# One 1024-column tile for the decays of all eight heads, and one two-bank PSUM tile for both score banks

## The chip, the cores and the metric

The kernel runs on one core of a Trainium2 chip. The metric is the device time of one execution in microseconds (us); the time before is 815.35 us, the median of 3 runs (815.07 to 815.9).

## What is computed

An mLSTM attention over 4 batches, 8 heads, 768 positions and head size 40, and behind it two feed-forward layers over its 3072 tokens of 320 numbers (2048 hidden units).

```python
for t in range(S):                                  # attention, per batch and head
    m_new  = maximum(f_gate[t] + m, i_gate[t])
    f_stab = exp(f_gate[t] + m - m_new); i_stab = exp(i_gate[t] - m_new); m = m_new
    C = f_stab * C + i_stab * outer(v[t], k[t])
    n = f_stab * n + i_stab * k[t]
    y[t] = sigmoid(o_gate[t]) * (C @ q[t]) / maximum(abs(n @ q[t]), 1.0)
x = y.transpose(0, 2, 1, 3).reshape(3072, 320)
h = x @ moe_w_in;  x = (h - tanh(h)) @ moe_w_out    # layer 0
h = x @ moe2_w_in                                   # layer 1: 0 below -1, h above 1,
g = where(h >= 1, h, where(h <= -1, 0, (h + 1) ** 2 / 4))   # a parabola between
out = g @ moe2_w_out
```

## The kernel before

The sequence is cut into chunks of 128 positions. A **job** n = 0 to 23 is one chunk c = n // 4 of one batch b = n % 4, with all 8 heads in two halves u = 0, 1 of four heads (512 columns). The 24 jobs make six blocks of four; block k of the first feed-forward layer needs the results of jobs 4k to 4k+3. Each layer runs 6 blocks of 16 **steps**; a step f multiplies the block's 512 columns by 128 hidden units (L650, `h`), applies the activation (L668 ACT tanh, L669 DVE subtraction, L681 ACT rounding to `gh`, L682 DVE remainder `gl`), and two steps later (LAG) multiplies the result into four accumulators (L702, `a`). In block 0 the first eight steps use plain fp32 matmuls (L640). Jobs of later blocks are interleaved with the steps of layer 0.

What a job does, in order: it loads q and k (`qkraw`), k, v and o (`nat`) and, for jobs 4 and later, the row of decay factors of each head broadcast over 128 partitions (`fb`, two DMAs of 256 KB); L460 turns each half of `fb` into a 128x128 matrix of decays per head by a scan against repeated identity matrices (`scan_id`), into a buffer `d`; L463 copies the last column of each to `wc`, which POOL (L506) multiplies into k; PE makes the scores of the two halves (`t_s`, L473 for jobs below 12, L489 from 12 on, where L484 and L486 first split q and k into two parts, through one buffer `xf`, one half at a time); L493 multiplies each bank of scores by its half of `d`; L520 multiplies q, scaled by `gb` on POOL (L510, L512), by the running state `C` into `t_n`; L529 adds the scores times v; L536 to L546 normalise; L551 transposes into `t_x`; L601 to L606 (`split_x`) leave the result in two parts for layer 0; L558 makes the new outer products `t_c`, L566 to L575 the new state.

PSUM has eight banks: two with the tag `h` for the steps, four accumulators `a0` to `a3`, and `tn` and `tb`. From job 4 on a job uses `tn` for `s0`, `n` and `x` one after the other and `tb` for `s1` and `c`; the gates' small transpose `t_i` (L370) takes `tn`. In layer 1 four steps run as a group whose `h` banks are h, h, `tn` and `tb`. `fb` has two buffers of 512 columns and `d` three.

The order of instructions on every engine is fixed when the program is built, by a list planner (`Plan`) with its own costs. Each operation has an engine, a cost in ns and a priority (`prio`, a lower one first); the planner always places the operation that can start earliest, and among those of one engine that could start within 150 ns of it the one of lowest priority. A buffer or bank of a tag comes free when its last user has ended, and is given out in the order in which the program asks for it. Operations with `lock` don't overlap in the plan, since DVE and POOL share a port. All loads go through the queue of SP, in order: a load that waits for its buffer holds those behind it. A job of block k has the priority 16(k-1) + 4(n mod 4) - 6 + s for its stage s, a step the number of the step, a step's activations that number less 3.5.

Of the kernel before, what the change touches and what calls it, by code (L numbers as in the profile page):

```python
# [7 lines left out]
F32 = mybir.dt.float32  # L8
# [10 lines left out]
L = 128  # L19
# [35 lines left out]
FFN = 4  # L55
STACK = 12
GS = 4
HTAGS = ["h", "h", "tn", "tb"]


class Buf:
# [14 lines left out]
class Plan:  # L76
# [20 lines left out]
    def op(self, eng, ns, prio, fn, r=(), w=(), out=None, lock=False):  # L97
        o = Op()
        o.eng, o.ns, o.prio, o.fn, o.seq, o.out = eng, ns, prio, fn, len(self.ops), out
        o.allocs, o.preds, o.succs = [], set(), []  # L100
        o.bufs, o.fill, o.lock = [], 0, lock
        key = lambda x: x if isinstance(x, tuple) else (x, None)

        for x in map(key, r):
# [3 lines left out]
        for x in map(key, w):  # L108
# [5 lines left out]
        for b in {key(x)[0] for x in (*r, *w)}:  # L114
# [99 lines left out]
def dve(n):  # L214
    return 157 + n / 0.96
# [16 lines left out]
def mlstm_moe_moe(ctx: ExitStack, tc: tile.TileContext, ig, fg, qk, qk3, q3, nat, w1, w2, cst, out):  # L232
# [7 lines left out]

    cs = const.tile([128, C_W], F32, name="cs")
    ident = cs[:, C_ID:C_ID + 128]
    scan_id = const.tile([128, 512], F32, name="scan_id")
    scan_bf = scan_id.bitcast(BF16)
# [32 lines left out]
    BANKS = {"h": 2}  # L277

    def bank(tag, name):
        return P.buf(of(ps), [128, 512], F32, tag, name, BANKS.get(tag, 1))  # L280

    def load(prio, dst, src, kb, r=(), w=(), rows=None, eng="SP"):

# [56 lines left out]
    def gates(g, prio):  # L340
        ca, cb = GROUPS[g]
        n = (cb - ca) * L
        cols = slice(ca * L, cb * L)
        if g == 0:
            fr, i_sb, m_sb, gr = (wbuf(NF - 1 - i, [128 if i == 0 else B * H, 2 * L + 1], F32, "gate0") for i in range(4))
        else:
            fr, i_sb, m_sb, gr = (abuf(t, [B * H, L + 1], F32, 1) for t in ("fr", "ig", "mg", "gr"))
        gt[g] = fr, gr
        ld = prio - 4 if g else -99
        load(ld, lambda: fr[0:32, 0:n], lambda: fg[:, cols], n / 8, w=[fr], rows=n * 4)  # L350
        load(ld, lambda: i_sb[0:32, 0:n], lambda: ig[:, cols], n / 8, w=[i_sb], rows=n * 4, eng="ACT" if g == 0 else "SP")
        op("DVE", 60, prio, lambda: nc.vector.tensor_copy(m_sb[:, 0:1], carry[:, g:g + 1]), [("carry", g)], [m_sb])
        op("DVE", dve(2 * n), prio, lambda: nc.vector.tensor_tensor_scan(
            out=m_sb[:, 1:n + 1], data0=fr[0:32, 0:n], data1=i_sb[:, 0:n],
            initial=carry[:, g:g + 1], op0=ALU.add, op1=ALU.max), [fr, i_sb, m_sb, ("carry", g)], [m_sb])
        if g + 1 < len(GROUPS):
            op("DVE", 60, prio, lambda: nc.vector.tensor_copy(carry[:, g + 1:g + 2], m_sb[:, n:n + 1]), [m_sb], [("carry", g + 1)])
        for o, d, f in ((fr, 0, ALU.add), (fr, 1, ALU.subtract), (i_sb, 1, ALU.subtract)):
            def part(e, o=o, d=d, f=f):
                z = o[0:32, 0:n]  # L360
                e.tensor_tensor(out=z, in0=z, in1=m_sb[:, d:n + d], op=f)

            vec(prio, n, part, [o, m_sb], [o])
            if d:
                x = op("ACT", act(n) + (1283 if o is fr and g else 0), prio, lambda o=o: nc.scalar.activation(o[0:32, 0:n], o[0:32, 0:n], AF.Exp), [o], [o])
                if g == 0:
                    exps.append(x)
        t = bank("h" if g == 0 else "tn", "t_i")
        for c in range(cb - ca):
            op("PE", pe(32), prio, lambda c=c: nc.tensor.transpose(  # L370
                t[:, c * 32:c * 32 + 32], i_sb[:, c * L:(c + 1) * L], ident[:32, :32]), [i_sb, "cs"], [t])
        op("DVE", dve(32 * (cb - ca)), prio, lambda: nc.vector.tensor_copy(
            isT[:, ca:cb, :], t[:, 0:(cb - ca) * 32].rearrange("p (c h) -> p c h", h=32)), [t], [("isT", g)])
# [3 lines left out]
    def decays(g, prio):  # L377
# [14 lines left out]
        load(max(prio, -60), lambda: fr_d[:, cols], lambda: fr[0:32, z], 16, [fr], [("fr_d", g)], rows=512)  # L392
        load(max(prio, -60), lambda: gr_d[:, cols], lambda: gr[:, z], 16, [gr], [("gr_d", g)], rows=512)

    def jbank(n, what, name):

        tag = {"s0": "tn", "s1": "tb", "n": "tn", "x": "tn", "c": "tb", "f": "h"}[what]
        if n < FIRST and what in "s0s1xc":
            tag = (("a3", "tb"), ("a0", "a1"))[n % 2][what in ("s1", "x")]
        return bank(tag, name)  # L400


    Cst = {}
# [2 lines left out]
    def job(n, at, ld):  # L406
# [14 lines left out]
        kc = group[c]  # L421
        f = {}
        if n >= FIRST:
            for u in range(2):
                ft = abuf("fb", [128, HU, L], F32, 2)
                load(ld + 0.5, lambda ft=ft: ft.t, lambda u=u: fr_d[
                    b * H + u * HU:b * H + (u + 1) * HU, c * L:(c + 1) * L].unsqueeze(0).to_broadcast([128, HU, L]),
                    256, r=[("fr_d", kc)], w=[ft], rows=512)
                f[u] = lambda ft=ft: ft.t.rearrange("p h t -> p (h t)"), ft
        if c > 0:  # L430
            g = abuf("gb", [120, 3, L], F32, 2)
            for i in range(3):
# [9 lines left out]
        dk = {}  # L442
        d0 = wbuf(6 + n % 2, [128, 1024], F32, "d0") if n < FIRST else None
        wc = abuf("wc", [128, H], F32, 2)
        for u in range(2):
            p = at(0) if u == 0 else at(1)
            if n < FIRST:
                ft = jbank(n, "f", "t_f")
                for h in range(HU):
                    r = b * H + u * HU + h  # L450
                    op("PE", 2 * pe(L, 128, 2), p, lambda h=h, r=r, ft=ft: nc.tensor.matmul(
                        ft[:, h * L:(h + 1) * L], ident[:, r:r + 1].to_broadcast([128, 128]),
                        gt[0][0][:, 0:L], start=True, stop=True), [gt[0][0], (gt[0][0], "z", 32), (gt[0][0], "z", 64), "cs"], [ft])
                f[u] = lambda ft=ft: ft.t, ft
            if d0 is None:
                d = abuf("d", [128, 512], F32, 3)
                dk[u] = lambda d=d: d.t, d
            else:
                dk[u] = lambda u=u: d0[:, u * 512:(u + 1) * 512], (d0, u)
            op("DVE", dve(1024), p, lambda o=dk[u][0], i=f[u][0]: nc.vector.tensor_tensor_scan(  # L460
                out=o(), data0=i(), data1=scan_id, initial=0.0, op0=ALU.mult, op1=ALU.add), [f[u][1], "scan_id"], [dk[u][1]], lock=n >= FIRST)
# [17 lines left out]
        else:  # L479
            for u in range(2):  # L480
# [7 lines left out]
                for h in range(HU):  # L488
                    op("PE", pe(L), at(u + 0.5), lambda u=u, t=t, h=h: nc.tensor.matmul(  # L489
                        sp[u][:, h * L:(h + 1) * L], t[:, 512 + h * L:512 + (h + 1) * L],  # L490
                        t[:, h * L:(h + 1) * L], start=True, stop=True), [t], [sp[u]])
        for u in range(2):
            op("DVE", dve(512), at(2 + u), lambda p=sp[u], d=dk[u][0]: nc.vector.tensor_tensor(  # L493
                out=d(), in0=p.t, in1=d(), op=ALU.mult), [sp[u], dk[u][1]], [dk[u][1]])

# [279 lines left out]
    def reload(f, prio):  # L775
# [157 lines left out]
```

## Time and profile before

| | |
|---|---|
| median of 3 runs | 815.35 us (815.07 to 815.9) |
| the profiled execution | 814.9 us, its span 813.1 us |
| PE (TensorE matmul) busy | 803.5 us, 99% of the span |
| DVE, ACT, POOL busy | 570.3, 429.6, 147.5 us |
| granted clock of TensorE | 1.000 |

The span runs from the first to the last instruction; the profiled execution took 1.8 us more than its span. Jobs 0 to 3 and the first loads fill about the first 33 us, layer 0 with the later jobs lies between 33 and about 460 us, layer 1 behind it. A busy PE is not a PE at its peak, since matmuls are pipelined and their ends are modelled; how far it is from waiting is read from the stretch between the starts of successive groups of matmuls.

### The profile page before, as it was taken

To read this page: it belongs to the slowest core of one execution; us is meant where nothing else is said; L and a number is where in the kernel's file an instruction comes from. 1 tells how busy PE (TensorE), PEld (TensorE's weight loads), DVE (VectorE), ACT (ScalarE), POOL (GpSimd) and SP (SyncE) were. 2 spreads that over 40 slices of the span, in tenths; PEclk is the share of its full clock that TensorE was granted. 3 is DMA by queue.
4 is the path that set the end of the run, shared out by engine and by line. 5 is a ranking of instruction groups with operands and counts; after the bars stand their busy time and mean duration, and the time that the engine had idled before them with its cause. 6 is when DMAs were issued, how large, how long until landed. Compare 5 with 4: busy or idle time off the path is not lost.

```text
span 813.1 us, 15218 instructions
## 1 busy us (share of the span) xinstructions
PE 803.5 (99%) x6030; PEld 692.8 (85%) x6034; DVE 570.3 (70%) x922; ACT 429.6 (53%) x810; POOL 147.5 (18%) x147
## 2 busy tenths in 40 slices
PE   9999999999999999999999999999999999999998
PEld 6656888888898888888899888898888889898887
DVE  6899989878888998887456684554646555564644
ACT  4866775675586677544455553443525435342432
POOL 3242122314234335332110200200200201000000
PEclk9999999999999999999999999999999999999999
DMA  8888356686758768771543120100100000000000
GB/s 263 311 261 271 101 194 175 165 260 160 202 164 243 206 188 230 214 178 45 150 116 100 53 72 1 40 33 1 40 33 1 32 1 1 33 1 1 34 1 32
DMA packets 62980, 93.66 MB, mean 115 GB/s; under 512 B 4701, under 2 KB 45501, under 8 KB 62909
## 3 DMA queue, kind: packets, MB, share of 16 engines
q1 hardware_dynamic: 62860, 92.66, 39.2%
q8 instruction: 47, 0.77, 0.4%
q14 instruction: 25, 0.20, 0.1%
q10 hardware_dynamic: 48, 0.03, 0.0%
HBM read 78.88 MB, written 13.80 MB: 114 GB/s over the span
## 4 chain that ended last, share of the span: by engine, by line
PE 90%; DMA 3%; DVE 2%; issue 1%; ACT 1%; SPq 1%; POOL 0%; POOLq 0%; ACTq 0%
PE a L702 40%; PE h L650 37%; PE h L640 3%; PE t_n L529 2%; PE h L629 2%; PE t_n L520 1%; PE t_s L473 1%; PE t_c L558 1%; PE t_s L489 1%; DMA nat<-in_nat_dram 1%; PE t_x L551 1%; DMA w_d<-w 1%; SPq L286 1%; DMA gb<-gr_d 1%; DMA fr_d<-fr 0%
## 5 line engine op out<-in xcount | busy, mean ns | idle before, releaser
L650 PE MATMUL h<-x,w 128*128 128x512 f32 x1376 | 350.1, 397 | 0.1
L702 PE MATMUL a<-w,gh 128*128 128x320 f32 x1472 | 329.3, 310 | 0.0
L650 PEld LDWEIGHTS h<-x,w 128*128 128x128 f32 x1376 | 249.5, 188 | 52.2 <-issue 6.8
L702 PEld LDWEIGHTS a<-w,gh 128*128 128x128 f32 x1472 | 250.0, 188 | 11.0 <-ACT ob L725 1.8
L702 PE MATMUL a<-w,gl 128*128 128x320 f32 x736 | 227.5, 310 | 0.0
L673 DVE TENSOR_SCALAR g<-h 128x512 f32<-128x512 f32 x96 | 63.7, 684 | 114.1 <-PE h L650 114.1
L675 ACT ACTIVATE g<-g,half 128x512 f32<-128x512 f32 x96 | 67.0, 721 | 135.5 <-DVE g L673 135.0
L702 PEld LDWEIGHTS a<-w,gl 128*128 128x128 f32 x736 | 138.2, 188 | 0.3
L669 DVE TENSOR_TENSOR h<-h,g 128x512 f32<-128x512 f32 x88 | 61.2, 695 | 44.0 <-ACT g L668 43.9
L677 DVE TENSOR_TENSOR g<-h,g 128x512 f32<-128x512 f32 x96 | 64.7, 692 | 27.1 <-ACT g L675 26.1
L681 ACT CAST gh<-g 128x512 fp32r<-128x512 f32 x96 | 59.5, 622 | 44.3 <-DVE g L677 43.6
L668 ACT ACTIVATE g<-h 128x512 f32<-128x512 f32 x88 | 52.5, 597 | 53.4 <-PE h L650 52.8
L766 POOL TENSOR_TENSOR x<-xl,x 128x512 fp32r<-128x512 f32 x18 | 25.0, 1420 | 278.1 <-ACT x L757 278.1
L681 ACT CAST gh<-h 128x512 fp32r<-128x512 f32 x88 | 51.4, 585 | 45.3 <-DVE h L669 45.0
L682 DVE TENSOR_TENSOR gl<-h,gh 128x512 fp32r<-128x512 f32 x88 | 60.1, 683 | 19.1 <-ACT gh L681 17.3
L682 DVE TENSOR_TENSOR gl<-g,gh 128x512 fp32r<-128x512 f32 x96 | 62.1, 687 | 4.0 <-ACT gh L681 1.2
L460 DVE TENSOR_TENSOR_SCAN d<-fb,scan_id 128x512 f32<-128x512 f32 x40 | 54.6, 1376 | 1.9 <-DMA fb<-fr_d 1.8
L486 POOL TENSOR_TENSOR xf<-qkraw,xf 120x1024 fp32r<-120x1024 f32 x12 | 32.6, 2713 | 38.1 <-ACT xf L484 34.4
L484 ACT ACTIVATE xf<-qkraw,cs 120x512 fp32r<-120x512 f32 x48 | 32.5, 716 | 6.1 <-PE t_s L489 6.0
L493 DVE TENSOR_TENSOR d<-t_s,d 128x512 f32<-128x512 f32 x48 | 32.0, 681 | 4.4 <-PE t_s L489 2.9
L539 POOL TENSOR_TENSOR nat<-nat,dn 128x320 f32<-128x320 f32 x24 | 21.0, 874 | 70.3 <-DVE dn L538 70.3
L500 POOL TENSOR_TENSOR nat<-nat,isT 128x328 f32<-128x328 f32 x24 | 22.6, 952 | 57.9 <-DMA nat<-in_nat_dram 37.2
(103 smaller groups left out, 765.2 us busy)
## 6 DMA issues: line engine op xcount, KB each, us to landing
w<-in_w_dram SPq DMA_DIRECT2D x32, 703.6 KB
nat<-in_nat_dram SPq DMA_DIRECT2D x24, 484.0 KB
qkraw<-in_qk_dram SPq DMA_DIRECT2D x24, 480.0 KB
fb<-fr_d SPq DMA_DIRECT2D x40, 256.0 KB
w_d<-w SPq DMA_DIRECT2D x16, 352.0 KB
w<-w_d SPq DMA_DIRECT2D x16, 352.0 KB
qkraw<-in_qk_dram SPq DMA_DIRECT2D x24, 160.0 KB
xr_d<-xo SPq DMA_DIRECT2D x24, 160.0 KB
```

What stands on the lines that cost most here:

```text
L460: op("DVE", dve(1024), p, lambda o=dk[u][0], i=f[u][0]: nc.vector.tensor_tensor_scan(out=o(), data0=i(), data1=scan_id, initial=0.0, op0=A ...
L484: op("ACT", act(512, 1), at(u - 1), lambda raw=raw, t=t, z=z, cols=cols: nc.scalar.activation(t[:, cols], raw[:, cols], AF.Copy, scale=cs[ ...
L486: vec(at(u - 1), 1024, lambda e, raw=raw, t=t: e.tensor_tensor(out=t.t, in0=raw.t, in1=t.t.bitcast(F32), op=ALU.subtract), [raw, t], [t], ...
L650: op("PE", pe(n), prio, lambda i=i, c=c, s=s: nc.tensor.matmul(p[:, :n], w[:, c:c + 128], x[:, s, :n], start=(i == 0 and not layer), stop= ...
L668: op("ACT", act(n), prio + 0.5 - FFN, lambda: nc.scalar.activation(t[:, :n], p[:, :n], AF.Tanh), [p], [t])
L669: op("DVE", dve(n), prio + 0.5 - FFN, lambda: nc.vector.tensor_tensor(out=p[:, :n], in0=p[:, :n], in1=t[:, :n], op=ALU.subtract), [p, t], [p])
L673: op("DVE", dve(n), prio + 0.5 - FFN, lambda: nc.vector.tensor_scalar(t[:, :n], p[:, :n], -1.0, 1.0, op0=ALU.max, op1=ALU.min), [p], [t])
L675: op("ACT", act(n, 1), prio + 0.5 - FFN, lambda: nc.scalar.activation(t[:, :n], t[:, :n], AF.Square, bias=half[:, 0:1], scale=0.5), [t, "h ...
L677: op("DVE", dve(n), prio + 0.5 - FFN, lambda: nc.vector.tensor_tensor(out=t[:, :n], in0=p[:, :n], in1=t[:, :n], op=ALU.max), [p, t], [t])
L681: op("ACT", act(n), prio + 1 - FFN, lambda: nc.scalar.copy(gh[:, :n], y[:, :n]), [y], [gh])
L682: op("DVE", dve(n), prio + 1 - FFN, lambda: nc.vector.tensor_tensor(out=gl[:, :n], in0=y[:, :n], in1=gh[:, :n].bitcast(F32), op=ALU.subtra ...
L702: op("PE", pe(DM) if gl is not None else 2 * pe(DM, 128, 2), prio, lambda A=A, r=r, a=a, c=c, i=i, dt=dt: nc.tensor.matmul(A[:, 0:DM], a[: ...
```

## The change

For jobs 4 and later the two `fb` buffers become one tile of 1024 columns (`fb`, still two of them, still loaded by two DMAs, one for each half). One scan of 1024 columns replaces two of 512, and writes its result over its input, so that the buffers `d` fall away for these jobs; `scan_id` is 1024 columns wide, its second half made by one more POOL copy. One copy of the eight last columns to `wc` replaces two of four. The PSUM tags `tn` and `tb` become one tag `t`, a tile of two banks; the class `Half` stands for one of its banks, and one tile serves a job from its scores to its last use. One DVE product of 1024 columns reads both banks of scores and replaces two. `place` keeps the order between operations for each half by itself. Jobs 0 to 3 keep their scans and products; the banks that were `tn` and `tb` are for them the halves of one tile. In layer 1 the third and fourth `h` of a group are the halves of one tile; `t_i` takes a whole tile.

```diff
+class Half:
+    def __init__(self, buf, i):
+        self.buf, self.i = buf, i
+    @property
+    def t(self):
+        return self.buf.t[:, self.i * 512:self.i * 512 + 512]
+def place(x):
+    x = x if isinstance(x, tuple) else (x, None)
+    return (x[0].buf, x[0].i, *x[1:]) if isinstance(x[0], Half) else x
...
-        return P.buf(of(ps), [128, 512], F32, tag, name, BANKS.get(tag, 1))
+        return P.buf(of(ps), [128, 1024 if tag == "t" else 512], F32, tag, name, BANKS.get(tag, 1))
...
-        t = bank("h" if g == 0 else "tn", "t_i")
+        t = bank("h" if g == 0 else "t", "t_i")
...
-        tag = {"s0": "tn", "s1": "tb", "n": "tn", "x": "tn", "c": "tb", "f": "h"}[what]
-        if n < FIRST and what in "s0s1xc":
-            tag = (("a3", "tb"), ("a0", "a1"))[n % 2][what in ("s1", "x")]
-        return bank(tag, name)
+        if what == "f":
+            return bank("h", name)
+        if n < FIRST and (n % 2 or what in "s0c") and what != "n":
+            return bank(("a3", "a0", "a1")[n % 2 + (what in ("s1", "x"))], name)
+        k = max(n, FIRST - 1)
+        if k not in pair:
+            pair[k] = bank("t", "t_j")
+        return Half(pair[k], int(what in ("s1", "c") or n < FIRST and what == "x"))
...
+            fb = abuf("fb", [128, 2 * HU * L], F32, 2)
             for u in range(2):
-                ft = abuf("fb", [128, HU, L], F32, 2)
-                load(ld + 0.5, lambda ft=ft: ft.t, lambda u=u: fr_d[
+                load(ld + 0.5, lambda u=u: fb[:, u * 512:u * 512 + 512].rearrange("p (h t) -> p h t", t=L), lambda u=u: fr_d[
...
+        if n >= FIRST:
+            for u in range(2):
+                dk[u] = lambda u=u: fb[:, u * 512:u * 512 + 512], (fb, u)
+            op("DVE", dve(2048), at(0), lambda: nc.vector.tensor_tensor_scan(
+                out=fb.t, data0=fb.t, data1=scan_id, initial=0.0, op0=ALU.mult, op1=ALU.add), [(fb, 0), (fb, 1), "scan_id", "scan_id2"], [(fb, 0), (fb, 1)], lock=True)
+            if not last:
+                op("ACT", 205, at(0) + 0.3, lambda: nc.scalar.copy(
+                    wc.t, fb.t.rearrange("p (h t) -> p h t", t=L)[:, :, L - 1]), [(fb, 0), (fb, 1)], [(wc, 0), (wc, 1)])
-        for u in range(2):
+        for u in range(2 if n < FIRST else 0):
...
-        for u in range(2):
+        if n >= FIRST:
+            op("DVE", dve(1024), at(2.5), lambda: nc.vector.tensor_tensor(
+                out=fb.t, in0=sp[0].buf.t, in1=fb.t, op=ALU.mult), [*sp, (fb, 0), (fb, 1)], [(fb, 0), (fb, 1)])
+        for u in range(2 if n < FIRST else 0):
             op("DVE", dve(512), at(2 + u), lambda p=sp[u], d=dk[u][0]: nc.vector.tensor_tensor(
...
+        two = bank("t", "h")
         for j in range(GS):
-            hb[f + j] = bank(HTAGS[j], "h")
+            hb[f + j] = bank("h", "h") if j < 2 else Half(two, j - 2)
...
+    op("POOL", 630, -20, lambda: nc.gpsimd.tensor_copy(
+        scan_id[:, 512:1024].rearrange("p (h t) -> p h t", t=L), ident.unsqueeze(1).to_broadcast([128, HU, L])),
+       ["cs"], ["scan_id2"])
```

## Rows read from the trace of the kernel before

**Rows 1.** The page: busy time and share of the span.
```profile
PE 803.5 (99%) x6030; PEld 692.8 (85%) x6034; DVE 570.3 (70%) x922; ACT 429.6 (53%) x810; POOL 147.5 (18%) x147
```

**Rows 2.** The chain in order of time: start us, us, what.
```profile
394.47 1.86 PE h L650 x8
396.33 1.75 PE a L702 x12
```

**Rows 3.** Busy time by windows: stretch, length, PE, PEld, DVE, ACT, POOL.
```profile
40.00:80.00 40.00, 38.97 (x301) 24.71 (x299) 39.50 (x55) 25.42 (x53) 13.10 (x15) 1.00 0.88 269
```

**Rows 4.** Groups of instructions by line: busy us, mean ns, idle before.
```profile
L493 DVE TENSOR_TENSOR d<-t_s,d 128x512 f32<-128x512 f32 x48 | 32.0, 681 | 4.4 <-PE t_s L489 2.9 <-PE t_s L473 0.6 <-ACT wc L463 0.5
...
L520 PE MATMUL t_n<-C,q 120*128 120x123 f32 (+1 forms) x120 | 16.2, 270 | 0.8 <-POOL q L510 0.7 <-issue 0.2
...
L602 DVE TENSOR_TENSOR x<-xf,x 128x1024 fp32r<-128x1024 f32 x1 | 1.2, 1219 | 0.0
```

**Rows 5.** The scan's line: count, shortest/median/longest ns.
```profile
L460 DVE TENSOR_TENSOR_SCAN d<-fb,scan_id x40: 1172/1224/2166, 45.9 to 376.1; 128x512 f32<-128x512 f32 x40
```

**Rows 6.** Timeline around a scan inside a step's activations: start us, us.
```profile
269.94 0.60 ACT L668 ACTIVATE g<-h 128x512 f32<-128x512 f32 x1
...
271.26 0.66 DVE L669 TENSOR_TENSOR h<-h,g 128x512 f32<-128x512 f32 x1
...
271.84 1.56 DVE L460 TENSOR_TENSOR_SCAN d<-fb,scan_id 128x512 f32<-128x512 f32 x1
271.95 0.59 ACT L681 CAST gh<-h 128x512 fp32r<-128x512 f32 x1 [0.58 <-DVE h L669]
273.31 0.66 DVE L682 TENSOR_TENSOR gl<-h,gh 128x512 fp32r<-128x512 f32 x1
...
274.03 0.30 PEld L650 LDWEIGHTS h<-x,w 128*128 128x128 f32 x2 [0.36 <-DVE gl L682]
```

**Rows 7.** Timeline of a late job's PSUM banks.
```profile
382.00 0.28 DVE L606 TENSOR_TENSOR x<-t_x,x 64x128 fp32r<-64x128 f32 x1
...
382.43 0.63 PE L489 MATMUL t_s<-xf 120*128 120x128 f32 x4
...
383.82 0.69 DVE L493 TENSOR_TENSOR d<-t_s,d 128x512 f32<-128x512 f32 x1
...
384.71 0.80 PE L520 MATMUL t_n<-C,q 120*128 120x123 f32 x6
...
386.68 0.69 DVE L493 TENSOR_TENSOR d<-t_s,d 128x512 f32<-128x512 f32 x1 [0.34 <-PE t_s L489]
387.54 0.69 PEld L529 LDWEIGHTS t_n<-nat,d 128*32 128x32 f32 x64 [0.36 <-issue]
```

**Rows 8.** Timeline: a block's last result, and the block's first step.
```profile
258.10 0.28 DVE L606 TENSOR_TENSOR x<-t_x,x 64x128 fp32r<-64x128 f32 x1
...
261.60 0.45 PE L650 MATMUL h<-x,w 128*128 128x512 f32 x1
...
331.35 0.28 DVE L606 TENSOR_TENSOR x<-t_x,x 64x128 fp32r<-64x128 f32 x1
...
336.06 0.63 PE L650 MATMUL h<-x,w 128*128 128x512 f32 x2
```

**Rows 9.** Windows of L650 alone: stretch, length, PE busy (matmuls).
```profile
190.50:261.50 71.00, 35.10 (x128) 22.50 (x128) 1.00 0.70 196
261.50:336.00 74.50, 35.64 (x128) 22.58 (x129) 1.00 0.74 203
```

**Rows 10.** Timeline: PE waits ahead of L520.
```profile
185.42 0.87 PE L520 MATMUL t_n<-C,q 120*128 120x123 f32 x6 [0.68 <-POOL q L510]
```

**Rows 11.** The SP queue's waits: us in total, times, longest.
```profile
SPq L286 <- DVE d L460: 27.4, 21, 3.2
```

**Rows 12.** Timelines of POOL and DVE in the first 50 us.
```profile
8.72 0.74 POOL L500 TENSOR_TENSOR nat<-nat,isT 128x328 f32<-128x328 f32 x1 [4.82 <-DMA nat<-in_nat_dram]
...
45.92 3.77 DVE L460 TENSOR_TENSOR_SCAN d<-fb,scan_id 128x512 f32<-128x512 f32 x2
```

More of the change, by code (lines that the diff above doesn't have):

```diff
@@ L57 @@
 GS = 4
-HTAGS = ["h", "h", "tn", "tb"]
 class Buf:
@@ L69, in __getitem__ @@
         return self.t[key]
+class Half:
[4 more added lines that the diff above has]
+        return self.buf.t[:, self.i * 512:self.i * 512 + 512]
+    def __getitem__(self, key):
+        return self.t[key]
+def place(x):
+    x = x if isinstance(x, tuple) else (x, None)
+    return (x[0].buf, x[0].i, *x[1:]) if isinstance(x[0], Half) else x
 class Op:
@@ L101, in op @@
         o.bufs, o.fill, o.lock = [], 0, lock
-        key = lambda x: x if isinstance(x, tuple) else (x, None)
-        for x in map(key, r):
+        for x in map(place, r):
             if x in self.last:
@@ L107, in op @@
             self.read.setdefault(x, []).append(o)
-        for x in map(key, w):
+        for x in map(place, w):
             if x in self.last:
@@ L113, in op @@
         o.preds.discard(o)
-        for b in {key(x)[0] for x in (*r, *w)}:
+        for b in {place(x)[0] for x in (*r, *w)}:
             if isinstance(b, Buf):
@@ L242, in mlstm_moe_moe @@
     ident = cs[:, C_ID:C_ID + 128]
-    scan_id = const.tile([128, 512], F32, name="scan_id")
-    scan_bf = scan_id.bitcast(BF16)
+    scan_id = const.tile([128, 2 * HU * L], F32, name="scan_id")
     isT = const.tile([128, NC, B * H], F32, name="isT")
@@ L393, in decays @@
         load(max(prio, -60), lambda: gr_d[:, cols], lambda: gr[:, z], 16, [gr], [("gr_d", g)], rows=512)
+    pair = {}
     def jbank(n, what, name):
-        tag = {"s0": "tn", "s1": "tb", "n": "tn", "x": "tn", "c": "tb", "f": "h"}[what]
-        if n < FIRST and what in "s0s1xc":
-            tag = (("a3", "tb"), ("a0", "a1"))[n % 2][what in ("s1", "x")]
-        return bank(tag, name)
+        if what == "f":
[6 more added lines that the diff above has]
+        return Half(pair[k], int(what in ("s1", "c") or n < FIRST and what == "x"))
     Cst = {}
@@ L423, in job @@
         if n >= FIRST:
+            fb = abuf("fb", [128, 2 * HU * L], F32, 2)
             for u in range(2):
-                ft = abuf("fb", [128, HU, L], F32, 2)
-                load(ld + 0.5, lambda ft=ft: ft.t, lambda u=u: fr_d[
+                load(ld + 0.5, lambda u=u: fb[:, u * 512:u * 512 + 512].rearrange("p (h t) -> p h t", t=L), lambda u=u: fr_d[
                     b * H + u * HU:b * H + (u + 1) * HU, c * L:(c + 1) * L].unsqueeze(0).to_broadcast([128, HU, L]),
-                    256, r=[("fr_d", kc)], w=[ft], rows=512)
-                f[u] = lambda ft=ft: ft.t.rearrange("p h t -> p (h t)"), ft
+                    256, r=[("fr_d", kc)], w=[(fb, u)], rows=512)
         if c > 0:
@@ L444, in job @@
         wc = abuf("wc", [128, H], F32, 2)
-        for u in range(2):
-            p = at(0) if u == 0 else at(1)
[L447 to L459, printed above, removed]
+        if n >= FIRST:
[6 more added lines that the diff above has]
+                    wc.t, fb.t.rearrange("p (h t) -> p h t", t=L)[:, :, L - 1]), [(fb, 0), (fb, 1)], [(wc, 0), (wc, 1)])
@@ new lines, in job @@
+        for u in range(2 if n < FIRST else 0):
+            p = at(0) if u == 0 else at(1)
+            ft = jbank(n, "f", "t_f")
+            for h in range(HU):
+                r = b * H + u * HU + h
+                op("PE", 2 * pe(L, 128, 2), p, lambda h=h, r=r, ft=ft: nc.tensor.matmul(
+                    ft[:, h * L:(h + 1) * L], ident[:, r:r + 1].to_broadcast([128, 128]),
+                    gt[0][0][:, 0:L], start=True, stop=True), [gt[0][0], (gt[0][0], "z", 32), (gt[0][0], "z", 64), "cs"], [ft])
+            f[u] = lambda ft=ft: ft.t, ft
+            dk[u] = lambda u=u: d0[:, u * 512:(u + 1) * 512], (d0, u)
@@ L460, in job @@
             op("DVE", dve(1024), p, lambda o=dk[u][0], i=f[u][0]: nc.vector.tensor_tensor_scan(
-                out=o(), data0=i(), data1=scan_id, initial=0.0, op0=ALU.mult, op1=ALU.add), [f[u][1], "scan_id"], [dk[u][1]], lock=n >= FIRST)
+                out=o(), data0=i(), data1=scan_id[:, 0:512], initial=0.0, op0=ALU.mult, op1=ALU.add), [f[u][1], "scan_id"], [dk[u][1]])
             if not last:
@@ L786, in mlstm_moe_moe @@
     op("POOL", 630, -97, lambda: nc.gpsimd.tensor_copy(
-        scan_id.rearrange("p (h t) -> p h t", t=L), ident.unsqueeze(1).to_broadcast([128, HU, L])),
+        scan_id[:, 0:512].rearrange("p (h t) -> p h t", t=L), ident.unsqueeze(1).to_broadcast([128, HU, L])),
        ["cs"], ["scan_id"])
+    op("POOL", 630, -20, lambda: nc.gpsimd.tensor_copy(
+        scan_id[:, 512:1024].rearrange("p (h t) -> p h t", t=L), ident.unsqueeze(1).to_broadcast([128, HU, L])),
+       ["cs"], ["scan_id2"])
     wz = gbuf("gh", [128, 512], F32, LAG + 1)
```

## The prediction

> **What bounds the kernel now.** First the busy times: PE has work in 99% of the span [rows 1]. Then the chain in order of time: in layer 0 a step is one group of eight L650 matmuls, 1.86 us, and one of twelve L702 matmuls, 1.75 us, each beginning where the other ends [rows 2]. The reader is to see that 3.61 us for a step holds no wait: PE's own instructions set the time, and the change removes none of them. What can be won is only waits of PE; what can be lost is new ones. The Trainium skill (Trainium Kernel Development and Optimization, Best Practices) calls the busy share of matmuls a poor measure of how near an engine is to its limit, so the first view alone would not have done; here both agree.
>
> So I looked for those, in three places. One: a step's activations. Between the end of a step's L650 group and the L650 group two steps on, which needs the same `h` bank, PE has 1.75 + 1.86 + 1.75 = 5.36 us of work [rows 2]. The four activation instructions take 0.60 + 0.66 + 0.59 + 0.66 = 2.51 us [rows 6]; 2.85 us are spare, less where a job's matmuls change the order. Two: the job chain. The next job's scores start 0.15 us after the last split of the job before has left the bank (382.00 + 0.28 to 382.43) [rows 7]; five more of the late jobs follow the one before as closely. The late jobs are thus a chain of their own, about as long as the stretch that they must fit in. Three: what that chain leaves. The L650 matmuls counted by windows put the first step of block 3 at 261.60 and that of block 4 at 336.06, each after a full 128 of the block before [rows 9]; the last splits that these blocks wait for end at 258.38 and 331.63, so 3.2 and 4.4 us are left [rows 8].
>
> **The change, part by part.** *Scan.* A scan of 512 columns takes 1.22 us in the median [rows 5]; two are 2.45. No row has one of 1024. From above it costs 2.45. A DVE product of 1024 columns took 1.22 us where one of 512 takes 0.68, twice of which is 1.36 [rows 4]: the second instruction's fixed part, 0.14, is what one long instruction saves. I take the same for the scan: 2.45 - 0.14 = 2.31 us. DVE gains 0.14 for each of 20 jobs by the scan.
>
> *Product.* Two of 0.68 become one of 1.22 [rows 4]: another 0.14. Together 0.28 us x 20 = 5.6 us of DVE work, and one ACT copy a job fewer. On PE's path this is worth nothing as long as the steps' spare of 2.85 us covers DVE; between 0 and the rival below.
>
> *Holding DVE for 2.31 us at a time.* A short scan that falls between a step's subtraction and its remainder already made PE wait: L669 ended at 271.92, the scan took 271.84 to 273.40, L682 came behind it, and PE's weight load waited 0.36 us [rows 6]. I saw that once for 40 scans. The scan ran 1.56 us there; one of 2.31 would make it 0.36 + 0.75 = 1.11. With the normal spare of 2.85 us, a long scan at that place delays the remainder by 2.31 - 0.59 (the ACT rounding runs meanwhile) = 1.72 us, and is hidden. I take one place of 1.1 instead of one of 0.36: +0.7 us. Bounds: -0.4 (no such meeting), and +3.7 (five of the 20 scans, 0.75 more each).
>
> *The port.* Two scans beside POOL's work took 3.77 us instead of 2.45 [rows 12], 1.3 more, and the longest single one 2.17 [rows 5]: DVE and POOL hinder each other in scans now, and as much scanning is left. The Trainium skill (SBUF — State Buffer, Who interferes with whom) has it that a DVE instruction with two SBUF inputs and a POOL instruction that reads SBUF exclude each other for a whole instruction, whoever starts first; the stretch above agrees. By that rule a scan twice as long makes a POOL instruction that meets it wait up to 2.31 us instead of 1.22; were L539 of every job to meet one, 1.1 us would come on top of the job chain's growth below. By the rows alone, with the same total of scanning, I take nothing.
>
> *Scores, product, `t_n`.* Before, L520 can start once the first half's product has read `tn`: at 384.71, two microseconds ahead of the second product at 386.68, behind which only L529 remains [rows 7]. Now `t_n`'s bank is read by the one product, which needs both scores. From job 12 on the chain after the second scores grows by the longer product, 1.22 - 0.69 = 0.53, and by L520, which moves behind it: 0.80 in its merged row [rows 7], of which the last matmul's 0.27 [rows 4] overlaps what follows: between 0.53 and 0.80, I take 0.65. The two are 1.2 us a job. For jobs 4 to 11, whose halves are scored together, only the part of L520 that ran beside the second product is added, at most 0.68. Cover: the 3.2 and 4.4 us left ahead of blocks 3 and 4 [rows 8]. If the jobs of a block take the growth out of its own margin, 4 x 1.2 = 4.8 against 3.2 leaves 1.6 us of wait; jobs that fall behind, however, stand ahead of steps by their priority, and win queueing back. I take 0; bounds 0 and 8 x 1.2 - 4.4 = +5.2 (both blocks' growth, none won back).
>
> *L520's own wait.* PE waited 0.68 us ahead of L520 at 185.42 for POOL's product of q [rows 10], 0.7 in all for that reason [rows 4]. L520 now comes behind the product of both halves, when q has long been scaled: -0.7 us. Bounds -0.7 and 0.
>
> *One tile of two banks, released whole.* A next job's scores wait also for the state's L566 and L575 reading the other bank. The handover at 382.43 is tied to the split, in the other bank [rows 7]; zero, and where a reader of the state came later than the split, one DVE read of a bank, 0.68 [rows 4]. In layer 1 the group's first matmuls need all four banks before and after; zero.
>
> *Loads on the SP queue.* `fb` was freed by the scan of the job before, for which the queue stood 27.4 us, 21 times, the longest 3.2 [rows 11]; now it is freed by L529 of the job two before, which comes earlier in a chain of jobs one behind the other. The loads queued behind it (q, `gb`, `nat`, weights) come no later; zero, with a gain only where a load is late, as in the 0.68 above. The DMAs are as many.
>
> *The second POOL copy* of the identity lies in POOL's first 8.7 us, of which 4.82 are one wait for `nat` [rows 12]; zero. Jobs 0 to 3 keep their work.
>
> The sum, on the profiled execution's own 814.9 (span 813.1 and 1.8 around it): 814.9 - 0.7 + 0.7 = 814.9. That execution lies 0.45 below the median of the runs, so **815.4 us**: no change that can be measured. A run of this kernel differs from the median by up to 0.07%; 0.2%, 1.6 us, is about what can be told from no change.
>
> **Rivals.**
> - *The job chain becomes the bound (slower).* Place: the first L650 of blocks 3 and 4. Price: between 1.6 and 5.2 us as worked out, in the middle 3.4: 818.8 us. It decides once the growth not won back is over (3.2 + 1.6) / 4 = 1.2 us a job. For it: the handover within 0.15 us and the small margins [rows 7, 8]. Against it: of the margins' 3.2 and 4.4 nothing is used today, and a late job overtakes the steps.
> - *Long scans stand in the steps' way (slower).* Five or more meetings: +3.7 us on 814.9 - 0.7 + 0.45: 818.4. Against it: 1.72 is within 2.85 [rows 2, 6].
> - *DVE paces the early blocks (faster).* Between 40 and 80 us DVE is busy 39.50 of 40 [rows 3]. If it sets that pace through jobs 4 to 11, 8 x 0.28 = 2.3 us come back: 813.1. Against it: PE is busy 38.97 in the same window [rows 3], so at most 1.0 of the 40 us is open there to win.
> - *The halves aren't kept apart.* If matmuls into one bank of the tile wait for a reader of the other, each of the 24 groups of layer 1 pays at least one DVE read, 24 x 0.68 = 16 us [rows 4]: 831. Nothing in the trace before has a tile of two banks, so only a rest of doubt.
>
> **How the numbers follow.** No measurable change 0.48; job chain 0.20; long scans 0.08; halves tied 0.02; DVE's relief, with the waits that a new order happens to remove, 0.22. So faster 0.22, same 0.48, slower 0.30. An order written anew moves every wait of layer 0, so I don't make the range small: down to 812.8, the DVE rival and 0.3 of lost waits; up to 819.0, just over the middle of the job chain's bounds. About 0.1 is left out above (its upper half and the tied halves), and less below. The likeliest case's own range is 813.8 to 817.0.
>
> **What the profile after would show.** Right: L460 with 20 scans of 1024 columns at about 2.3 us, L493's successor near 1.22 and 20 of them, DVE some 5 us less busy, PE busy unchanged within 2 us, steps still 3.6 us, no PE wait for POOL's q. For the job chain: L520 directly behind the product and directly ahead of L529, the time from second scores to L529 1.2 us longer, and the last split still ahead of the first L650 of blocks 3 and 4; a wait there for a DVE or ACT split is the slower rival. A weight load of L650 waiting for the remainder in several jobs is the second. Wrong at the root would be: PE groups in layer 1 no longer back to back, or layer 0 ending several us earlier than 460 with no wait of the trace before to explain it.

## The result, and the profile after

The changed kernel takes 826.06 us (median of 4 runs, 825.14 to 826.42) against 815.21 us (4 runs) for the kernel before: ratio 1.0133, 95% interval [1.0116, 1.0149]. It is 1.3% slower; forecast was 815.4 us in a range of 812.8 to 819.0. The profiled execution of after took 825.14 us (span 823.4), that of before 814.9 (span 813.1): 10.3 us of span to explain. In the changed kernel L460 has become L468, L493 L516, L520 L546, L529 L555, the clamp of the denominator L536/L537 L562/L563, the transposes L551 L577, the outer products L558 L584, the state's copies L566/L570 L592/L596, `split_x` L606 L632, `h` L650 L677, `a` L702 L729.

First the busy times, then the chain of the steps, then groups by line (busy us, mean ns, idle before and its releasers).

```profile
PE 805.6 (98%) x6030; PEld 695.6 (84%) x6033; DVE 566.1 (69%) x882; ACT 428.6 (52%) x794; POOL 148.6 (18%) x148
```
```profile
91.42 1.75 PE a L729 x12
93.17 1.84 PE h L677 x8
```
```profile
L468 DVE TENSOR_TENSOR_SCAN fb<-fb,scan_id 128x1024 f32<-128x1024 f32 x20 | 46.7, 2334 | 2.8 <-DMA fb<-fr_d 2.4
L516 DVE TENSOR_TENSOR fb<-t_j,fb 128x1024 f32<-128x1024 f32 x20 | 24.3, 1217 | 5.1 <-PE t_j L512 3.8 <-PE t_j L496 0.7 <-ACT wc L471 0.4
...
L584 PE MATMUL t_j<-nat 128*120 128x123 f32 x64 | 11.6, 290 | 3.2 <-DVE dn L563 2.1 <-ACT t_j L562 0.8 <-DVE x L572 0.2
L577 PE MATMUL t_j<-cs,x 128*128 128x128 f32 x66 | 11.4, 277 | 2.1 <-DVE x L572 1.0 <-ACT t_j L596 0.5 <-ACT t_j L592 0.5
```

Everything that was sized is as sized: PE's work grew by 2 us only [rows 1], a step is still 1.84 + 1.75 us [rows 2], the long scan takes 2.33 us, the long product 1.22, VectorE is 4.2 us less busy. Yet PE idles 17.8 us of its span instead of 9.6: 8.2 of the 10.3 us. The last two rows show a new kind of wait: L584, which multiplies k and v into the second half of the two-bank tile (`t_j`), waits for VectorE's clamp L563 and ScalarE's |.| L562, which read the **first** half and have nothing to do with it; and the transposes into the first half wait for L592 and L596, which read the second. The state's copies L592, which read the second half, also stand 2.1 us for the transposes and 1.8 us for the clamp; their forerunners in the program before, L566, wait for PE's outer products alone.

One such place, in order of time (start us, us; a bracket is the idle time before it):

```profile
200.69 0.37 PE L584 MATMUL t_j<-nat 128*120 128x123 f32 x2
201.10 0.17 DVE L563 TENSOR_SCALAR dn<-t_j 128x8 f32<-128x8 f32 x1 [0.46 <-PE t_j L584]
...
201.32 0.46 PEld L584 LDWEIGHTS t_j<-nat 128*120 128x120 f32 x4 [0.45 <-DVE dn L563]
201.32 0.62 PE L584 MATMUL t_j<-nat 128*120 128x123 f32 x4 [0.26 <-DVE dn L563]
...
201.98 0.30 ACT L592 ACTIVATE t_j<-t_j,cs 120x82 f32<-120x82 f32 x1 [1.98 <-PE t_j L584]
```

Six matmuls of one job fall apart into two and four: the clamp waits for the first two, the other four wait for the clamp. The longest such wait, 1.57 us at 238.76, is PE behind a clamp that stood behind 2.63 us of another scan on VectorE's queue:

```profile
235.20 2.38 POOL L509 TENSOR_TENSOR xf<-qkraw,xf 120x1024 fp32r<-120x1024 f32 x1 [7.00 <-PE t_j L546]
235.22 2.63 DVE L400 TENSOR_TENSOR_SCAN gr<-fr,zero 32x128 f32<-32x128 f32 x1
...
237.96 0.67 DVE L709 TENSOR_TENSOR gl<-h,gh 128x512 fp32r<-128x512 f32 x1
...
238.56 0.14 DVE L563 TENSOR_SCALAR dn<-t_j 128x8 f32<-128x8 f32 x1
...
238.76 0.83 PE L584 MATMUL t_j<-nat 128*120 128x123 f32 x6 [1.57 <-DVE dn L563]
```

The length of this wait is not the tie's alone: the scan L400 took 0.36 to 0.41 us in its other three places, and 2.63 only here, beside POOL's L509.

### The profile page after: what moved, and what is told of

Same layout as the page of the kernel before. It is cut to its first block, busy times and chain, and to the rows that moved or that the text cites. A ratio compares the mean times of both kernels' runs of the same rounds, so it can differ in the third digit from the quotient of the medians.

```text
span 823.4 us, 15195 instructions
## 1 busy us (share of the span) xinstructions
PE 805.6 (98%) x6030; PEld 695.6 (84%) x6033; DVE 566.1 (69%) x882; ACT 428.6 (52%) x794; POOL 148.6 (18%) x148
## 4 chain that ended last, share of the span: by engine, by line
PE 86%; DMA 5%; DVE 3%; ACT 2%; issue 2%; SPq 1%; POOL 1%; POOLq 0%; ACTq 0%; DVEq 0%
PE a L729 37%; PE h L677 36%; PE t_j L555 2%; PE h L656 2%; DMA fb<-fr_d 2%; PE t_j L546 1%; PE t_j L584 1%; PE t_j L512 1%; PE t_f L478 1%; PE h L667 1%; PE t_j L496 1%; PE t_j L577 1%; DMA w<-in_w_dram 1%; PE spare L826 1%; DMA q<-in_q_dram 1%
## 5 line engine op out<-in xcount | busy, mean ns | idle before, releaser
L677 PE MATMUL h<-x,w 128*128 128x512 f32 x1376 | 345.7, 396 | 0.8 <-DVE g L700 0.8
L729 PE MATMUL a<-w,gh 128*128 128x320 f32 x1472 | 329.7, 311 | 0.3 <-ACT gh L708 0.3
L677 PEld LDWEIGHTS h<-x,w 128*128 128x128 f32 x1376 | 250.9, 188 | 54.4 <-issue 6.8
L729 PEld LDWEIGHTS a<-w,gh 128*128 128x128 f32 x1472 | 249.4, 188 | 11.2 <-ACT ob L752 1.9
L729 PE MATMUL a<-w,gl 128*128 128x320 f32 x736 | 226.6, 309 | 0.0
L700 DVE TENSOR_SCALAR g<-h 128x512 f32<-128x512 f32 x96 | 64.0, 686 | 113.4 <-PE h L677 113.3
L702 ACT ACTIVATE g<-g,half 128x512 f32<-128x512 f32 x96 | 67.1, 721 | 138.3 <-DVE g L700 137.9
L729 PEld LDWEIGHTS a<-w,gl 128*128 128x128 f32 x736 | 138.1, 188 | 0.4
L704 DVE TENSOR_TENSOR g<-h,g 128x512 f32<-128x512 f32 x96 | 64.7, 692 | 27.8 <-ACT g L702 26.4
L709 DVE TENSOR_TENSOR gl<-h,gh 128x512 fp32r<-128x512 f32 x88 | 60.3, 686 | 22.4 <-ACT gh L708 21.6
L709 DVE TENSOR_TENSOR gl<-g,gh 128x512 fp32r<-128x512 f32 x96 | 62.1, 686 | 3.6 <-ACT gh L708 0.7
L468 DVE TENSOR_TENSOR_SCAN fb<-fb,scan_id 128x1024 f32<-128x1024 f32 x20 | 46.7, 2334 | 2.8 <-DMA fb<-fr_d 2.4
L509 POOL TENSOR_TENSOR xf<-qkraw,xf 120x1024 fp32r<-120x1024 f32 x12 | 28.6, 2385 | 58.0 <-PE t_j L546 21.3
L335 ACT ACTIVATE cvb<-w,half 128x704 bf16<-128x704 int8 x32 | 29.9, 935 | 4.4 <-DVE w L337 2.2
L536 POOL TENSOR_TENSOR q<-q,gb 120x256 f32<-120x256 f32 x20 | 21.6, 1079 | 53.8 <-DMA gb<-gr_d 32.6
```

Of the source, the lines that this page charges most:

```text
L335: op("ACT", 935, prio, lambda o=o, y=y: nc.scalar.activation(o(), x(), AF.Relu, bias=rebase, scale=y * 2.0 ** 27), [t, "half"], [u if y > ...
L468: op("DVE", dve(2048), at(0), lambda: nc.vector.tensor_tensor_scan(out=fb.t, data0=fb.t, data1=scan_id, initial=0.0, op0=ALU.mult, op1=ALU ...
L677: op("PE", pe(n), prio, lambda i=i, c=c, s=s: nc.tensor.matmul(p[:, :n], w[:, c:c + 128], x[:, s, :n], start=(i == 0 and not layer), stop= ...
L700: op("DVE", dve(n), prio + 0.5 - FFN, lambda: nc.vector.tensor_scalar(t[:, :n], p[:, :n], -1.0, 1.0, op0=ALU.max, op1=ALU.min), [p], [t])
L702: op("ACT", act(n, 1), prio + 0.5 - FFN, lambda: nc.scalar.activation(t[:, :n], t[:, :n], AF.Square, bias=half[:, 0:1], scale=0.5), [t, "h ...
L704: op("DVE", dve(n), prio + 0.5 - FFN, lambda: nc.vector.tensor_tensor(out=t[:, :n], in0=p[:, :n], in1=t[:, :n], op=ALU.max), [p, t], [t])
```

## The experiments

**Theory (tied halves):** the framework that writes the semaphore waits keeps account of a PSUM tile as one thing. Every access to one half waits for the other half's last accesses by other engines, while the planner (`place`) takes the halves as apart and orders the operations so. This is called the tie below, and a kernel with two tiles of one bank in its place untied. **Rivals:** the long scan or the later `t_n` lengthens the job chain; or another order is slower by chance.

**One part alone.** The first run keeps the long scan and goes back to two banks and two products; the second keeps the two-bank tile and goes back to two scans and two products; the third is the change with two products.

```diff
 # scan alone: the banks of before
-        return P.buf(of(ps), [128, 1024 if tag == "t" else 512], F32, tag, ...)
+        return P.buf(of(ps), [128, 512], F32, tag, ...)
+        tag = {"s0": "tn", "s1": "tb", "n": "tn", "x": "tn", "c": "tb", "f": "h"}[what]
 # banks alone: the scans of before (per half, fb -> d)
+            op("DVE", dve(1024), p, ... tensor_tensor_scan(out=o(), data0=i(), data1=scan_id[:, 0:512], ...
 # all three: the products of before
-            op("DVE", dve(1024), at(2.5), lambda: nc.vector.tensor_tensor(
-                out=fb.t, in0=sp[0].buf.t, in1=fb.t, op=ALU.mult), ...
+        for u in range(2):
             op("DVE", dve(512), at(2 + u), ...
```

> The scan of 1024 columns in place and the single copy of the eight last columns, with the two score banks as two tiles and two products of 512 columns, as before the change. Tied halves (the two halves of the two-bank tile wait for each other, which the order written for the program does not reckon with): nothing is tied here, so the time is that of before within 2 us, 813 to 817 us, and the waits ahead of the state's matmuls and of the transposes are as few as before. Long scan (a scan of 2.33 us lengthens the job chain and holds DVE): most of the 11 us remain, 820 to 826 us. New order (any other order moves layer 0 by some us by chance): anywhere from 811 to 823 us.

> The two-bank tile alone: two scans and two products of 512 columns as before the change, but both scores, t_n, the transposes and the state in the halves of one tile, and layer 1's third and fourth bank too. Tied halves: most of the 11 us are here without any long scan or merged product, 821 to 826 us. Long scan or merged product: as before, 813 to 817 us. New order: 811 to 823 us.

> The changed kernel with two products of 512 columns instead of the one of 1024: the scan and the two-bank tile stay. Tied halves: the second half's scores and both products stay on one tile, so the loss stays, 822 to 827 us. If the merged product is what costs (t_n behind both scores, 1.2 us a job and 20 jobs), most comes back: 815 to 818 us. New order: 813 to 826 us.

Measured (ratio to the kernel before, with its 95% interval): the scan alone 816.04 us, ratio 1.0007 [0.9984, 1.003], as expected if the halves are tied; the banks alone 828.16, 1.0167 [1.0139, 1.0195], 2 us above that range; scan and banks with two products 835.42, 1.0253 [1.0221, 1.0285]. The loss goes with the two-bank tile and is there without any long scan. The third run was worse than the change, which none of the theories had said.

**The same order without the tie.** The planner still gives the tile out whole; when it is issued, it becomes two tiles of one bank, which the framework can also take back one by one.

```diff
-        return self.buf.t[:, self.i * 512:self.i * 512 + 512]
+        return self.buf.t[self.i]
...
+                if b.tag == "t":
+                    b.t = [b.pool().tile([128, 512], b.dtype, tag=f"t{i}", ...) for i in range(2)]
```

> The kernel of the run before (scan of 1024, two products of 512) with each two-bank tile made as two tiles of one bank, taken and given back at the same places: the order of every engine's instructions is the same, one by one; only the tie between the halves is gone. Tied halves: PE's waits ahead of the state's second matmul and of the transposes go, and with them most of the loss, 814 to 819 us. Long scan or an unlucky order: nothing changes against the run before, within 1 us, since both have the same order and the same scan.

Measured: 816.52 us, ratio 1.0007 [0.9986, 1.0028], 19 us less in the same order, as expected if the halves are tied. Here is the place at which the third run loses most, PE's `t_n` (L543) behind the two products (L516, one row of two); with the tie first, then without it (L545 and L518 there).

```profile
129.51 1.27 DVE L516 TENSOR_TENSOR fb<-t_j,fb 128x512 f32<-128x512 f32 x2
...
130.88 0.87 PE L543 MATMUL t_j<-C,q 120*128 120x123 f32 x6 [1.06 <-POOL nat L529]
```
```profile
119.65 1.29 DVE L518 TENSOR_TENSOR fb<-t_j,fb 128x512 f32<-128x512 f32 x2
...
120.48 0.83 PE L545 MATMUL t_j<-C,q 120*128 120x123 f32 x6
```

`t_n` goes into the first half, which the first product has read. Untied, PE starts it 0.83 us after the products began, while the second still runs; tied, 1.37 us after, as the second has ended. (The row names POOL as releaser, but L529 there writes k, which `t_n` doesn't read, and was done 0.24 us earlier.) Since both kernels issue the same 6030 matmuls in the same order, their starts can be subtracted one by one. Of 16.8 us in the profiled executions, `t_n` makes 5.9, the transposes 5.0, the outer products 2.5, the first 36 us 1.8, layer 1 1.9, all others together -0.3. In the change the order puts `t_n` behind the one product anyway, so the first of these hardly arises there. That this makes the third run the worst isn't shown: the banks alone have two products on a tied tile too, and in their order PE stood only 0.9 us ahead of `t_n` (L541).

**The change itself without the tie.** The same edit on the changed kernel, and the one product that would read two tiles written as two, back to back:

```diff
+            def product():
+                for u in range(2):
+                    nc.vector.tensor_tensor(out=dk[u][0](), in0=sp[u].t, in1=dk[u][0](), op=ALU.mult)
```

> The changed kernel's own order, instruction by instruction, with each two-bank tile made as two tiles of one bank; only the product of 1024 columns, which reads both, is written as two of 512, one directly behind the other in the same place (0.14 us more of VectorE per job). Tied halves: the loss goes without any change of the order, 813 to 818 us, and PE's starts, laid beside those of the changed kernel one by one, fall back at the state's matmuls and the transposes. Order, long scan or later t_n (they are all still here): 823 to 827 us.

Measured: 811.63 us (12 runs), ratio 0.9961 [0.9945, 0.9977], 1.4 us below the range expected for tied halves. Not only is the loss gone, this kernel is faster than the one before. The place shown above, and the two groups, now read:

```profile
194.59 0.15 DVE L568 TENSOR_SCALAR dn<-t_j 128x8 f32<-128x8 f32 x1
194.73 0.73 PE L589 MATMUL t_j<-nat 128*120 128x123 f32 x6
```
```profile
L582 PE MATMUL t_j<-cs,x 128*128 128x128 f32 x66 | 10.9, 275 | 0.3 <-DVE x L577 0.2
L589 PE MATMUL t_j<-nat 128*120 128x123 f32 x64 | 9.9, 277 | 0.0
```

The six matmuls run in one go, and of 3.2 and 2.1 us of idle time ahead of the two groups 0.0 and 0.3 are left. Subtracting PE's starts again, of 11.1 us (14.4 between the medians; the untied execution profiled is the slowest of its 12) 8.3 lie in layer 0 (outer products 5.7, of it seven places of 0.37 to 0.42 and one of 1.7, the place at 238.76; transposes 2.5; scores 1.2; `t_n` 1.2; 2.2 given back, where `h` matmuls of the untied kernel wait and those of after don't), 1.4 in the first 36 us, 1.4 in layer 1. The 1.2 of `t_n` are not the tie's: in after it starts 0.10 us behind the end of the one product, here it needs only the first of two. The 1.4 of the first 36 us go with a slower clock in after (last section). That leaves about 8.5 us for the tie itself: 7.1 in layer 0 and 1.4 in layer 1.

The scores come late because VectorE and ScalarE, too, wait for each other at the end of a job, one reading the new outer products in the second half (L601) and the other the transposed result in the first (L627, L631). In after:

```profile
136.03 0.34 DVE L601 SCALAR_TENSOR_TENSOR C<-C,gb,t_j 120x123 f32<-120x123 f32 x1 [0.39 <-ACT x L627]
136.40 0.26 ACT L631 CAST x<-t_j 64x128 fp32r<-64x128 f32 x1 [0.41 <-DVE C L601]
136.70 0.30 DVE L601 SCALAR_TENSOR_TENSOR C<-C,gb,t_j 80x82 f32<-80x82 f32 x1 [0.33 <-ACT x L631]
136.91 0.41 DVE L628 TENSOR_TENSOR x<-t_j,x 128x256 fp32r<-128x256 f32 x1
```

and in the untied kernel the same instructions side by side:

```profile
130.90 0.54 DVE L606 SCALAR_TENSOR_TENSOR C<-C,gb,t_j 120x123 f32<-120x123 f32 x2
130.92 0.37 ACT L632 CAST x<-t_j 128x256 fp32r<-128x256 f32 x1 [0.67 <-PE t_j L582]
...
131.19 0.26 ACT L636 CAST x<-t_j 64x128 fp32r<-64x128 f32 x1
131.48 0.42 DVE L633 TENSOR_TENSOR x<-t_j,x 128x256 fp32r<-128x256 f32 x1
```

**An order that knows of the tie.**

```diff
-    return (x[0].buf, x[0].i, *x[1:]) if isinstance(x[0], Half) else x
+    return (x[0].buf, None, *x[1:]) if isinstance(x[0], Half) else x
```

> The changed kernel as it is, but the program that writes the order counts both halves of a two-bank tile as one thing: an operation on one half is set behind the last writer and the readers of the other. The tie itself stays. If what costs is that the order did not reckon with the tie (PE and DVE stand at the head of their queues for a wait that the order put at zero), much of the 11 us comes back: 816 to 821 us, with fewer waits of PE ahead of the state's matmuls and the transposes. If the tie costs whatever the order (a job is longer by it and PE has nothing to put in its place), the time stays at 824 to 828 us.

> The order that counts both halves as one thing, with two tiles of one bank: the order of the run that took 837 us, without the tie. If that run was slow because its order holds operations back for the tie, it stays slow without it, 828 us or more. If it was slow through waits that the tie still makes, it comes back to 813 to 820 us.

Measured: 836.97 us, ratio 1.0292 [1.0258, 1.0326], outside both expectations; the same order untied 830.65, 1.0185 [1.0154, 1.0216], as expected of a slow order. So most of its loss is in its order, which puts operations of a job one behind the other that could overlap; its first matmul of layer 0 (L667) starts at 40.93 us instead of 35.06. In the profiled executions untying it changed nothing (spans 831.2 and 832.4), but these are the fastest of the four tied and the slowest of the four untied; the medians differ by 6 us. What of it the waits are stays open. Reckoning with the tie is no cure here.

**How much an order alone moves.** Four runs change one number of the planner, two in the kernel before, two in the untied kernel (whose scan is reckoned at `dve(2048) + 40`):

```diff
-            op("DVE", dve(1024), p, lambda ...: nc.vector.tensor_tensor_scan(
+            op("DVE", dve(1024) + 40, p, lambda ...: nc.vector.tensor_tensor_scan(
...
-    PATIENCE = 150.0
+    PATIENCE = 160.0
```

> The kernel before with nothing changed but the order: the cost that the order reckons for a scan is 40 ns higher. How much an order written anew moves the time by itself: if the 11 us could be an unlucky order, this differs from the kernel before by several us, up or down; by the tie, within 2 us: 813 to 817 us.

> The kernel before with another single number of the order's writer changed: an operation of higher rank may be chosen 160 ns after the earliest one instead of 150. As the run before: within 2 us (813 to 817 us) unless orders alone move the time by several us.

> The kernel of the same-order run (the change with separate tiles, 811.6 us) in another order: patience 160 ns instead of 150. If the 3.4 us that it won against the kernel before are VectorE's shorter work, they stay in any order: 809 to 813 us. If they were a lucky order, this comes out among the other untied orders, 814 to 818 us.

> As the run before, with another change of the order: the long scan is reckoned 40 ns dearer. VectorE's shorter work: 809 to 813 us. A lucky order: 814 to 818 us.

| kernel | order | us | ratio to before [95%] |
|---|---|---|---|
| before | scan 40 ns dearer | 817.82 | 1.0026 [1.0006, 1.0046] |
| before | patience 160 | 814.95 | 1.0004 [0.9982, 1.0027] |
| untied | as written | 811.63 | 0.9961 [0.9945, 0.9977] |
| untied | patience 160 | 817.47 | 1.0038 [1.0017, 1.0059] |
| untied | scan 40 ns dearer | 812.28 | 0.9973 [0.9953, 0.9994] |

Orders alone move the time of the untied kernel by 0.8%, between 811.6 and 817.5 us. Of the kernel before, one other order came out 0.8 us above the 813 to 817 us expected, one within. Orders can't make the 1.33% of the change, whose own order is the 811.6 one. But they leave open whether the untied kernel is faster because VectorE does less, or by its order: two of its three orders are faster than before and one is slower, and of the two last runs one came out as expected of the shorter work, the other as expected of a lucky order.

## Why the prediction was wrong

**One tile of two banks, released whole.** This is the step that failed. It looked only at the handover of the tile from job to job, and put it, and layer 1, at "zero". For the handover that isn't contradicted: in after no matmul of the scores is shown waiting for the state's readers in the other bank (the untied runs don't price it by itself, since two tiles can come free one by one). What the step left out are the waits *inside* a job, between the halves that one job uses side by side. Net, they make about 7.1 us of the 11.1 between the profiled executions of after and of the same order untied; layer 1 makes 1.4 more.

**The halves aren't kept apart.** The right mechanism stood among the rivals, with a chance of 0.02 and a price of 16 us for layer 1. The price was in the wrong place. In layer 1 the tie costs 1.4 us, all in the second group. At its start the third bank's first matmul waits for L704's reading of the fourth, which leaves a loss of 0.3 us; later the fourth step's last three matmuls wait for L700's reading of the third bank, 1.0 us:

```profile
483.50 0.18 PEld L656 LDWEIGHTS h<-x,w 64*128 64x128 f32 x1 [1.05 <-DVE g L704]
483.51 0.50 PE L656 MATMUL h<-x,w 64*128 64x512 f32 x1 [0.74 <-DVE g L704]
...
493.68 0.69 DVE L700 TENSOR_SCALAR g<-h 128x512 f32<-128x512 f32 x1 [0.26 <-PE h L677]
...
494.43 0.96 PE L677 MATMUL h<-x,w 128*128 128x512 f32 x3 [0.78 <-DVE g L700]
```

This is the one sign of being wrong at the root that the prediction named and that came: a group of layer 1 no longer back to back. Later groups find the activations long done: from the fourth group's first matmul to the last group's, before and after both take about 285.5 us. The tie costs where readers and writers of the two halves are close together in time, and these are the jobs of layer 0: `t_n`'s readers beside the outer products, the state's copies beside the transposes. The chance was low because no row of before had a tile of two banks; a missing row is no evidence for zero.

The Trainium skill (PSUM — Partial Sum Buffer, PSUM bank collisions raise a hardware error) has accesses by two engines run clean in different banks, and guards by bank. The untied runs agree: L545 above wrote one bank from 120.48 while VectorE read the other until 120.94. The waits of the change thus come from how the program keeps account of a tile; two tiles of one bank work without them.

**Right:** the scan (forecast 2.31 us, median 2.29, mean 2.33), the product (1.22), and the job chain. From the end of the second scores to L529 or L555 the twelve late jobs take 0.95 us before and 2.17 after in the median, 1.2 us more as forecast, and the cover holds. Of [rows 8] the margins are still there, 2.8 and 2.6 us from the last split to the block's first step, so the job chain is not the bound:

```profile
266.20 0.28 DVE L632 TENSOR_TENSOR x<-t_j,x 64x128 fp32r<-64x128 f32 x1
...
269.31 0.63 PE L677 MATMUL h<-x,w 128*128 128x512 f32 x2
...
340.75 0.28 DVE L632 TENSOR_TENSOR x<-t_j,x 64x128 fp32r<-64x128 f32 x1
...
343.64 0.62 PE L677 MATMUL h<-x,w 128*128 128x512 f32 x2
```

**Long scans in the steps' way:** forecast +0.7, from a wait of 0.36 us [rows 6] that only the weight load had: before, PE's idle time ahead of L650 is 0.1 us in all. In after no L677 waits for the remainder L709, but the untied kernel, in the same order, has the mechanism twice, 1.25 us and 0.55 us of PE's time:

```profile
181.36 2.29 DVE L470 TENSOR_TENSOR_SCAN fb<-fb,scan_id 128x1024 f32<-128x1024 f32 x1 [1.74 <-DMA fb<-fr_d]
...
183.57 0.67 DVE L714 TENSOR_TENSOR gl<-h,gh 128x512 fp32r<-128x512 f32 x1
...
184.29 0.97 PE L682 MATMUL h<-x,w 128*128 128x512 f32 x3 [1.25 <-DVE gl L714]
```

VectorE stood 1.74 us for the load of `fb` (1.08 at the other place) and then scanned, with the remainder behind both. The spare of 2.85 us did not cover a scan with a late load ahead of it. In after these two waits are absent (they are most of the 2.2 given back above); the scan alone has two of 0.2 us. So the mechanism is real, and of the size that was given for one meeting (1.11), but it is not what made the change slower.

**Scores, product, `t_n`:** taken at 0 with bounds to +5.2, it cost 1.2 us of PE's time, most of it at two places where `t_n` stands directly behind the product. **L546's own wait:** the 0.7 us for q [rows 10] went, and at these places two waits of together the same size came. The view names POOL's k and v, which `t_n` doesn't read; each time the one product had ended 0.1 us before:

```profile
PE t_j L546 <- POOL nat L526: 0.4, 1, 0.4
PE t_j L546 <- POOL nat L532: 0.3, 1, 0.3
```

**Loads:** the queue no longer waits for the scan (27.4 us [rows 11]), but longer for the buffer of q, which the later `t_n` frees: 43.4 us for L520 before, 61.3 for L546 after.

**DVE's relief:** 4.2 us less work rather than 5.6; of this the slow L400 above takes back 2.2. Between 40 and 80 us VectorE is busy 37.12 where it was 39.50 [rows 3]. Whether it set the pace there can't be read from after, whose first step of block 0's second half comes at 77.17 us instead of 77.39, since its layer 0 starts later (35.06 instead of 33.20) and has the tie. In the untied kernel of the same order that step comes at 74.74 us. From layer 0's first step to it the kernel before takes 44.2 us, its two other orders 42.2 and 42.8, the scan alone and the untied kernels 41.0 to 42.0. So this rival seems to have been right for that stretch, by up to 3 us; but block 1 starts at 113.0 us against 113.5 before, and little of it is left.

```profile
40.00:80.00 40.00, 39.38 (x287) 24.52 (x286) 37.12 (x49) 27.22 (x53) 13.94 (x15) 1.00 0.90 268
```

**The range.** Without the tie the change lies between 811.6 and 817.5 us by its order, which the range 812.8 to 819.0 nearly spans: as wide as the orders alone, with no room for a mechanism of its own.

## What to carry to other kernels

Merging two PSUM banks into one tile saves a little fixed cost on the instruction that reads both, and can tie everything else that uses the halves; whoever merges should first ask which engines work on the two halves at the same time, because each such pair can become a wait. Where an order is planned ahead, a dependency that the planner doesn't know makes PE wait at the head of its in-order queue, and a planner that knows of it can come out slower still (836.97 us here). To tell a wait from an order, issue the same order with the wait's cause removed and subtract the start times one by one.

## What the runs showed of the hardware

In the profiled execution of after TensorE's granted clock fell once, early on. PE was busy 2.35 us of the 4 from 16 us on; then the clock was 0.70 and 0.87 of its upper level, 2.4 GHz (the lower, 1.2 GHz, is 0.5, so it was there for a part of each stretch). Columns of the windows: stretch, length, PE, PEld, DVE, ACT, POOL, clock, DMA share, GB/s.

```profile
16.00:20.00 4.00, 2.35 (x73) 1.48 (x71) 2.69 (x4) 1.59 (x3) 1.12 (x2) 1.00 1.01 348
20.00:24.00 4.00, 4.00 (x31) 3.88 (x31) 2.27 (x6) 2.75 (x11) 1.82 (x2) 0.70 0.97 391
24.00:28.00 4.00, 4.00 (x95) 3.66 (x95) 3.96 (x8) 2.34 (x7) 0.70 (x2) 0.87 0.84 332
```
```profile
21.92 3.48 PE L478 MATMUL t_f<-gate,cs 128*128 128x128 f32 x16
```

Without the tie, the same sixteen matmuls of the same order took 1.99 us at the full clock, after a stretch with 2.66 us busy:

```profile
16.00:20.00 4.00, 2.66 (x68) 1.98 (x70) 3.71 (x5) 2.92 (x8) 1.40 (x2) 1.00 1.00 352
20.00:24.00 4.00, 4.00 (x54) 3.71 (x54) 3.40 (x7) 2.33 (x9) 2.75 (x3) 1.00 1.00 402
```
```profile
22.19 1.99 PE L480 MATMUL t_f<-gate,cs 128*128 128x128 f32 x16
```

The slower clock cost 1.5 us in these sixteen matmuls. It isn't what makes the change slower: two of its four runs have a mean clock of 1.000 and took 826.28 and 825.84 us, the two at 0.998 took 825.14 and 826.42. And single runs of the kernel before lay between 811.2 and 821.1 us on the chips used here, far wider than the first three runs (815.07 to 815.9) had suggested; differences of some tenths of a per cent need many runs side by side.
